# Keys and values of batches 2 to 7: half of each group of eight is added by an accumulating DMA from GpSimd

## The chip, the cores and the metric

The kernel runs on one core of a Trainium2 chip. The core has five engines that work side by side, each through its own instructions in program order: TensorE (PE, matrix products, with PEld for its weight loads), VectorE (DVE), ScalarE (ACT), GpSimd (POOL) and SyncE (SP). Semaphores order them against each other. Data travel between the chip's memory (HBM) and the on-chip SBUF by DMA; TensorE writes its products to PSUM, the second on-chip memory. The metric is the time of one execution in microseconds. Three runs of the kernel before took 1375.69, 1375.94 and 1376.54 us; their median, 1375.94, is the time before.

## What is computed

The reference is an attention whose keys and values are averaged over groups of eight positions, followed by two feed-forward layers. Cut to what matters:

```python
# q, k, v: 8 batches x 8 heads x 576 positions x 64
k_p = k.reshape(B, H, 72, 8, 64).mean(axis=3)
v_p = v.reshape(B, H, 72, 8, 64).mean(axis=3)
scores = q @ k_p.transpose(0, 1, 3, 2) / 8
attn = softmax(scores)                      # with 1e-9 in the denominator
x = (attn @ v_p)                            # as 4608 tokens x 512
h = x @ w_in                                # 512 x 2048
g = maximum(h, 0) + log1p(exp(-abs(h)))
x = g @ w_out                               # 2048 x 512
# second layer: each token goes to one of 8 experts (the largest of its logits)
out[mask] = gate * (maximum(x[mask] @ w1[e], 0) @ w2[e])
```

The sums over eight positions (`k_p`, `v_p`) are the part that the change is about. Each (head, pooled position) has 8 x 64 = 512 numbers that lie in HBM one after the other; the sum over the eight leaves 64.

## The kernel before, in words

The 4608 tokens are cut into nine blocks of 512. For each block, `mm1` multiplies by `w_in` in 16 chunks of 128 columns, `softplus` forms `g` on ScalarE and VectorE, and `mm2` multiplies by `w_out` into four PSUM accumulators. Each float32 product is made of three products of split halves (`three`, lines 656 to 658). The attention of a later batch runs between the chunks of an earlier block: transposes of queries (`Q`, line 321), scores (`S`, line 338, tile `pp`), transposes of the attention weights (`T`, lines 395 and 401, tiles `pm` and `pl`) and the products with the values (`AV`, lines 422 to 425, tile `pv`). In this stage the tiles `pq`, `pp`, `pm`, `pl` and `pv` share two PSUM buffers (tag `a`), so TensorE can begin one only when the one before the last has been read out.

Batches 0 and 1 are prepared in the first block, by a list of steps written out by hand (`ORDER`, line 1182). Batches 2 to 7 are prepared by a planner (`make_plan`), which puts steps into the gaps between the chunks of the blocks 1 to 8. Its steps for a batch are `FK` and `FV` (the loads of keys and values), `PK` (sum the keys over eight and multiply by two masks), `KT` (transpose them), `PV` and `PR` (sum the values) and `BV` (masks and splits of the values).

- A batch's keys are loaded by SyncE in three DMAs: two of 128 x 2 x 512 (`fetch_main`, line 225) and one of 64 x 512 with the rows that don't fit (`fetch_kl`, line 236). Its values take five: two of 128 x 2 x 512 (line 225) and three copies of 32 x 2 x 512 (`fetch_vl`, line 245).
- All go to a pool `stp` of three buffers (tag `st`). A buffer is loaded again only when the sums that read it are done; SyncE waits for that in its queue, and what is behind it in the queue waits too.
- VectorE sums over eight: `pool_sum`, line 186, one instruction for each of the eleven pieces of a batch: four of `ks`, one of `klm`, four of `vs`, two of `vl`. The two pieces of `vl` hold 96 rows, the one of `klm` 64.
- GpSimd multiplies by the masks (line 219, tiles `km`, `vm`, `vlm`), scales the attention weights (line 358, tile `e`), and in block 1 subtracts to split every other chunk of `w_out` (line 638, tile `wo`; VectorE has the rest). VectorE then spreads a part of `e` into `el` (line 369); both are transposed by TensorE.

TensorE and SyncE run in the order in which the program text issues their instructions. VectorE, ScalarE and GpSimd run, from block 1 on, in an order that a scheduler chose when the kernel was built; it is fixed in the program, and on the chip each engine keeps to it.

Of the kernel before, what the change touches and what calls it, by code (L numbers as in the profile page):

```python
# [9 lines left out]
F32 = mybir.dt.float32  # L10
# [3 lines left out]
ALU = mybir.AluOpType  # L14
AX = mybir.AxisListType
# [5 lines left out]
def tile_attention_moe_moe(  # L21
# [13 lines left out]
    nc = tc.nc  # L35
    P = 128
    B, H, S, D = q.shape
    POOL = 8
# [4 lines left out]
    NJ = H // 2  # L43
# [8 lines left out]
    PK = 2 * SP  # L52
# [8 lines left out]
    stp = ctx.enter_context(tc.tile_pool(name="stp", bufs=3))  # L61
# [121 lines left out]


    def pool_sum(dst, src, pin):
        ins = nc.vector.tensor_reduce(dst, src.rearrange("p (e d) -> p d e", e=POOL), AX.X, ALU.add)
        if pin:
            tc.keep_in_program_order(ins)

    def rows(a, b):  # L190
        return a[b].rearrange("h (s e) d -> (h s) (e d)", e=POOL)


    def stage(shape, dtype, early):
        if early:
            return wp.tile(shape, dtype, tag="W", name="st")
        return stp.tile(shape, dtype, tag="st", name="st")
# [10 lines left out]
    def add(dst, src, step):  # L208
        if alt(step):
            tree_sum(dst, src)  # L210
        else:
            pool_sum(dst, src, int(step[1:step.index(".")]) > 1)
# [7 lines left out]

    km_t, st_t, el_t = {}, {}, {}

    def fetch_main(a, b, i, early):
        st = stage([P, 2, POOL * D], F32, early)
        nc.sync.dma_start(st, rows(a, b).rearrange("(j r) c -> r j c", j=NJ)[0:P, 2 * i:2 * i + 2, :])
        return st

    def fetch_k(b, i):
        st_t["k", b, i] = fetch_main(k, b, i, b < 2)

    def fetch_v(b, i):
        st_t["v", b, i] = fetch_main(v, b, i, b < 2)

    def fetch_kl(b):
        st = stp.tile([P, POOL * D], F32, tag="st", name="st")
        nc.sync.dma_start(st[0:64, :], rows(k, b).rearrange("(j r) c -> r j c", j=NJ)[P:PK])
        st_t["kl", b] = st

    def fetch_vl(b):
        st = stp.tile([P, 2, POOL * D], F32, tag="st", name="st")
        src = rows(v, b).rearrange("(j r) c -> r j c", j=NJ)[P:PK]
        for i in range(3):
            nc.sync.dma_start(st[32 * i:32 * (i + 1)], src)
        for g in range(2):
            st_t["vl", b, g] = st[:, g, :]

# [279 lines left out]
    def emit_step(o):  # L528
        if o[0] == "T":
            run(atrans(o[1]))  # L530
        elif o[0] == "Q":
            t = o[1]
            if t + 1 < NTL:
                load_q(t + 1)
            run(qtrans(t))
        elif o[0] == "S":
            run(score(o[1]))
            run(spread(o[1]))
        elif o[0] == "FK":
            for i in range(2):  # L540
                fetch_k(o[1], i)
            fetch_kl(o[1])
        elif o[0] == "FV":
            for i in range(2):
                fetch_v(o[1], i)
            fetch_vl(o[1])
        elif o[0] in ("PK", "KT", "PV", "PR"):
            if o not in preps:
                preps[o] = {"PK": prep_k, "KT": kT, "PV": prep_v, "PR": prep_r}[o[0]](o[1])
            next(preps[o], None)  # L550
        elif o[0] == "AV":
            _, si, j = o
            run(av(si, j))
        elif o[0] == "BV":
            run(build_r(o[1]))
            run(build_v(o[1]))
# [615 lines left out]
    def loads(c, *a):  # L1172
        f = {"k": fetch_k, "l": fetch_kl, "v": fetch_v, "r": fetch_vl, "q": load_q, "i": fetch_in, "o": fetch_out}
        f[c](*a)
# [218 lines left out]
```

## Time and profile before

The profiled execution took 1376.53 us; its span, from the first to the last instruction, is 1374.70 us, so 1.83 us lie outside the span. It is 0.59 us above the median of the three runs.

| engine | busy, us | share of the span | instructions |
|---|---|---|---|
| PE | 1350.0 | 98% | 6998 |
| DVE | 763.5 | 56% | 1608 |
| ACT | 644.5 | 47% | 1287 |
| POOL | 281.4 | 20% | 268 |

The granted clock of TensorE is 0.996 of its full speed over the span. The chain of work that ended last lies on PE for 83% of the span, on DVE for 8%, on DMA for 3%. A busy share is an average over the span: what an engine's work is worth in one stage is seen only in that stage, by who waits for whom there. All 166.94 MB of DMA traffic but 1.22 MB of instruction code go through SyncE's queue; GpSimd issues none of it.

### The profile page before, as it was taken

The numbers are of one execution on the slowest core, as the hardware profiler recorded it, in microseconds if no ns is written. First come the engines' busy times: TensorE is split into PE (matmuls) and PEld (weight loads), VectorE is DVE, ScalarE is ACT, GpSimd is POOL, SyncE is SP. The second block draws the span as 40 slices with busy tenths as digits, with TensorE's granted clock in tenths as the row PEclk, the third lists the DMA queues.
The fourth block names the chain that finished last, engine by engine and source line by source line (L and its number), as shares of the span: only waits on it lengthen the run. The fifth ranks groups of instructions, "written<-read, shape, count | busy, mean of one in ns | idle before, by whom it ended". The sixth has DMA issues, their size and how long they took to land.

```text
span 1374.7 us, 18505 instructions
## 1 busy us (share of the span) xinstructions
PE 1350.0 (98%) x6998; PEld 1118.0 (81%) x6998; DVE 763.5 (56%) x1608; ACT 644.5 (47%) x1287; POOL 281.4 (20%) x268
## 2 busy tenths in 40 slices
PE   8999999999999999999999999999999999999998
PEld 7666678878888878888888888878878898998986
DVE  7997567566465466475564443353664544544432
ACT  5766455554465464564464454455532322222221
POOL 6500112121021020020020010073353022231100
PEclk9999999999999999999999999999999999999999
DMA  9742354353364363453442242563332212222000
GB/s 275 244 125 85 105 172 140 112 195 107 113 203 124 95 195 92 127 181 95 139 153 85 79 152 77 168 210 126 107 124 93 87 37 77 78 93 93 31 31 32
DMA packets 113564, 166.94 MB, mean 121 GB/s; under 512 B 42808, under 2 KB 69432, under 8 KB 113472
## 3 DMA queue, kind: packets, MB, share of 16 engines
q1 hardware_dynamic: 113472, 165.72, 38.2%
q8 instruction: 57, 0.93, 0.3%
q14 instruction: 35, 0.29, 0.1%
HBM read 128.99 MB, written 36.70 MB: 121 GB/s over the span
## 4 chain that ended last, share of the span: by engine, by line
PE 83%; DVE 8%; DMA 3%; POOL 2%; ACT 2%; issue 1%; SPq 1%; POOLq 0%; DVEq 0%; ACTq 0%
PE h L656 8%; PE h L658 8%; PE h L657 8%; PE acc L656 8%; PE acc L658 8%; PE acc L657 8%; PE y L656 5%; PE y L657 5%; PE y L658 5%; PE m L656 4%; PE m L658 4%; PE m L657 4%; PE pp L338 2%; PE acc L710 2%; PE lg L742 1%; DMA wos<-wo 1%
## 5 line engine op out<-in xcount | busy, mean ns | idle before, releaser
L656 PE MATMUL h<-x,wi 128*128 128x512 f32 x576 | 234.9, 408 | 1.2 <-DVE t L689 1.1
L658 PE MATMUL h<-x,wi 128*128 128x512 f32 x576 | 225.7, 392 | 0.0
L657 PE MATMUL h<-x,wi 128*128 128x512 f32 x576 | 225.0, 391 | 0.0
L672 ACT ACTIVATE t<-h 128x512 f32<-128x512 f32 x144 | 86.1, 598 | 229.5 <-PE h L658 222.7
L656 PE MATMUL acc<-g,ring 128*128 128x512 f32 x448 | 177.9, 397 | 0.1
L658 PE MATMUL acc<-g,ring 128*128 128x512 f32 x448 | 174.8, 390 | 0.0
L657 PE MATMUL acc<-g,ring 128*128 128x512 f32 x448 | 174.4, 389 | 0.0
L689 DVE SCALAR_TENSOR_TENSOR t<-h,t 128x512 f32<-128x512 f32 x128 | 87.9, 687 | 147.3 <-ACT t L676 146.1
L656 PEld LDWEIGHTS h<-x,wi 128*128 128x128 f32 x576 | 108.7, 189 | 24.4 <-DVE t L689 1.8
L658 PEld LDWEIGHTS h<-x,wi 128*128 128x128 f32 x576 | 108.4, 188 | 24.2
L657 PEld LDWEIGHTS h<-x,wi 128*128 128x128 f32 x576 | 108.8, 189 | 21.1 <-issue 1.0
L691 ACT CAST g<-t 128x512 fp32r<-128x512 f32 x128 | 79.6, 622 | 86.7 <-DVE t L689 86.6
L693 DVE TENSOR_TENSOR g<-t,g 128x512 fp32r<-128x512 f32 x128 | 92.0, 719 | 50.7 <-ACT g L691 50.6
L656 PE MATMUL y<-w,g 128*128 128x512 f32 x288 | 113.0, 392 | 0.0
L657 PE MATMUL y<-w,g 128*128 128x512 f32 x288 | 112.9, 392 | 0.0
L658 PE MATMUL y<-w,g 128*128 128x512 f32 x288 | 112.9, 392 | 0.0
L658 PEld LDWEIGHTS acc<-g,ring 128*128 128x128 f32 x448 | 84.1, 188 | 18.4
L656 PEld LDWEIGHTS acc<-g,ring 128*128 128x128 f32 x448 | 84.2, 188 | 16.2 <-issue 0.6
L657 PEld LDWEIGHTS acc<-g,ring 128*128 128x128 f32 x448 | 84.2, 188 | 15.8
L358 POOL TENSOR_TENSOR e<-e,sm 128x576 f32<-128x576 f32 x34 | 39.4, 1159 | 270.9 <-DVE sm L355 223.5
L676 ACT ACTIVATE t<-t 128x512 f32<-128x512 f32 x144 | 91.4, 635 | 2.9
L674 ACT ACTIVATE t<-t 128x512 f32<-128x512 f32 x144 | 91.5, 636 | 2.1
(228 smaller groups left out, 2713.9 us busy)
## 6 DMA issues: line engine op xcount, KB each, us to landing
ring<-wos SPq DMA_DIRECT2D x112, 512.0 KB, 3.7
x2s<-x SPq DMA_DIRECT2D x9, 2048.0 KB, 8.3
b<-x2s SPq DMA_DIRECT2D x27, 512.0 KB, 5.2
out_dram<-o SPq DMA_DIRECT2D x36, 256.0 KB, 2.1
st<-in_k_dram SPq DMA_DIRECT2D x16, 512.0 KB, 5.1
q<-in_q_dram SPq DMA_DIRECT2D x32, 256.0 KB, 4.3
st<-in_v_dram SPq DMA_DIRECT2D x16, 512.0 KB, 6.7
st<-in_moe_w_in_dram SPq DMA_DIRECT2D x16, 512.0 KB, 7.0
```

The lines of the kernel that those rows point to most:

```text
L338: nc.tensor.matmul(pp[p0:p0 + n, i, :], qT[:, j, p0:p0 + n], kbd_t[b][:, j, :], start=True, stop=True)
L358: eng.tensor_tensor(e, e, sm1.unsqueeze(2).to_broadcast([P, H, SP]), ALU.mult)
L656: nc.tensor.matmul(ps, ll, rh, start=first, stop=False, skip_group_check=more)
L657: nc.tensor.matmul(ps, lh, rl, start=False, stop=False, skip_group_check=more)
L658: nc.tensor.matmul(ps, lh, rh, start=False, stop=last, skip_group_check=more)
L672: nc.scalar.activation(t, h, AF.Abs)
L674: nc.scalar.activation(t, t, AF.Exp, scale=-1.0)
L676: nc.scalar.activation(t, t, AF.Ln, bias=1.0)
L689: nc.vector.scalar_tensor_tensor(t, h, 0.0, t, ALU.max, ALU.add)
L691: nc.scalar.copy(g[:, 0, :], t)
L693: nc.vector.tensor_tensor(g[:, 1, :], t, f32(g)[:, 0, :], ALU.subtract)
L710: nc.tensor.matmul(accs[blk][d], wof[fc][:, dd], f32(g)[:, 0, :], start=first, stop=(fc == NFC - 1))
```

## The change

For batches 2 to 7 each staging buffer is half as wide. SyncE loads the first four of each eight positions into it (256 numbers for a row). When these have landed, GpSimd issues a second DMA that reads the other four positions from HBM and adds them in SBUF to what lies there (`accum_op=ALU.add`). VectorE sums four values instead of eight. Batches 0 and 1 are loaded and summed as before. The view in `pool_sum` is written by its inner size (`d=D`), so that it takes four or eight.

```diff
     def pool_sum(dst, src, pin):
-        ins = nc.vector.tensor_reduce(dst, src.rearrange("p (e d) -> p d e", e=POOL), AX.X, ALU.add)
+        ins = nc.vector.tensor_reduce(dst, src.rearrange("p (e d) -> p d e", d=D), AX.X, ALU.add)
...
+    HALF = POOL * D // 2
+
+    def added(dst, src):
+        nc.sync.dma_start(dst, src[..., 0:HALF])
+        nc.gpsimd.dma_start(dst, src[..., HALF:], accum_op=ALU.add)
+
     def fetch_main(a, b, i, early):
-        st = stage([P, 2, POOL * D], F32, early)
-        nc.sync.dma_start(st, rows(a, b).rearrange("(j r) c -> r j c", j=NJ)[0:P, 2 * i:2 * i + 2, :])
+        st = stage([P, 2, POOL * D if early else HALF], F32, early)
+        src = rows(a, b).rearrange("(j r) c -> r j c", j=NJ)[0:P, 2 * i:2 * i + 2, :]
+        if early:
+            nc.sync.dma_start(st, src)
+        else:
+            added(st, src)
         return st
...
     def fetch_kl(b):
-        st = stp.tile([P, POOL * D], F32, tag="st", name="st")
-        nc.sync.dma_start(st[0:64, :], rows(k, b).rearrange("(j r) c -> r j c", j=NJ)[P:PK])
+        st = stp.tile([P, POOL * D if b < 2 else HALF], F32, tag="st", name="st")
+        src = rows(k, b).rearrange("(j r) c -> r j c", j=NJ)[P:PK]
+        if b < 2:
+            nc.sync.dma_start(st[0:64, :], src)
+        else:
+            added(st[0:64, :], src)
         st_t["kl", b] = st
...
     def fetch_vl(b):
-        st = stp.tile([P, 2, POOL * D], F32, tag="st", name="st")
+        st = stp.tile([P, 2, POOL * D if b < 2 else HALF], F32, tag="st", name="st")
         src = rows(v, b).rearrange("(j r) c -> r j c", j=NJ)[P:PK]
         for i in range(3):
-            nc.sync.dma_start(st[32 * i:32 * (i + 1)], src)
+            if b < 2:
+                nc.sync.dma_start(st[32 * i:32 * (i + 1)], src)
+            else:
+                added(st[32 * i:32 * (i + 1)], src)
```

A batch then has eight accumulating DMAs on GpSimd, 48 in all. Lines after the change stand 17 higher from line 268 on (358 is 375, 638 is 655, 693 is 710); the new DMAs are lines 226 (SyncE) and 227 (GpSimd). TensorE's and SyncE's instructions keep their order. The scheduler's orders of the other three change at a few places.

The first place is GpSimd's queue where the values of batch 3 are fetched. Before, it holds the masks of the keys, two pieces of `w_out` and one tile of attention weights:

```order
L358 TENSOR_TENSOR e_2105<-e_2105,sm_2118 128x576
L219 TENSOR_SCALAR km_2279<-ks_2210,hm 128x4x64 x2
L638 TENSOR_TENSOR wo_2323<-wof_123,wo_2323 128x512
L358 TENSOR_TENSOR e_2281<-e_2281,sm_2294 128x576
L638 TENSOR_TENSOR wo_2465<-wof_123,wo_2465 128x512
```

Now, in the same place (`e_2105` is `e_2116`, `e_2281` is `e_2292`; numbers behind a name count buffers):

```order
L375 TENSOR_TENSOR e_2116<-e_2116,sm_2129 128x576
L219 TENSOR_SCALAR km_2290<-ks_2221,hm 128x4x64 x2
L227 DMA st<-in_v_dram 128x2x256 x2
L655 TENSOR_TENSOR wo_2334<-wof_123,wo_2334 128x512
L227 DMA st<-in_v_dram 32x2x256 x3
L375 TENSOR_TENSOR e_2292<-e_2292,sm_2305 128x576
L655 TENSOR_TENSOR wo_2481<-wof_123,wo_2481 128x512
```

Two accumulating DMAs now stand ahead of a piece of `w_out`, and three more ahead of the attention weights `e_2292`.

The second place is VectorE's queue where the values of batch 2 are summed, at the end of a token block's routing. Before:

```order
L799 RECIPROCAL gate_all<-n 128x4
L638 TENSOR_TENSOR wo_1957<-wof_122,wo_1957 128x512
L186 TENSOR_REDUCE vs_1821<-st 128x64
L693 TENSOR_TENSOR g<-t,g 128x512
L186 TENSOR_REDUCE vs_1821<-st 128x64
L438 TENSOR_TENSOR x_1905<-pv,x_1905 128x128 x3
```

Now:

```order
L816 RECIPROCAL gate_all<-n 128x4
L710 TENSOR_TENSOR g<-t,g 128x512
L186 TENSOR_REDUCE vs_1829<-st 128x64
L655 TENSOR_TENSOR wo_1965<-wof_122,wo_1965 128x512
L186 TENSOR_REDUCE vs_1829<-st 128x64
L455 TENSOR_TENSOR x_1913<-pv,x_1913 128x128 x3
```

The subtraction that ends `g` has changed places with the piece of `w_out`; the same two sums stand ahead of the read-out of `pv`.

The third place is GpSimd's queue where the keys of batch 4 are fetched. Before:

```order
L219 TENSOR_SCALAR vlm_3140<-vl_2787,lm 96x128 x2
L219 TENSOR_SCALAR vm_3145<-vs_2648,hm 128x4x64 x2
L768 TENSOR_TENSOR n<-lt,half 128x4
L358 TENSOR_TENSOR e_2932<-e_2932,sm_2945 128x576
L358 TENSOR_TENSOR e_3097<-e_3097,sm_3110 128x576
```

Now:

```order
L219 TENSOR_SCALAR vlm_3159<-vl_2803,lm 96x128 x2
L219 TENSOR_SCALAR vm_3164<-vs_2664,hm 128x4x64 x2
L227 DMA st<-in_k_dram 128x2x256 x2
L227 DMA st<-in_k_dram 64x1x256
L785 TENSOR_TENSOR n<-lt,half 128x4
L375 TENSOR_TENSOR e_2951<-e_2951,sm_2964 128x576
L375 TENSOR_TENSOR e_3116<-e_3116,sm_3129 128x576
```

The three accumulating DMAs of the keys stand behind the masks of the values of batch 3, and ahead of a routing step. The batches 5 to 7 look alike.

## Rows read from the trace of the kernel before

**Rows 1.** Busy time by stretch: start and end, length, engines, clock, DMA share, GB/s.

```profile
133.00:725.00 592.00, 587.12 (x2862) 474.94 (x2861) 351.76 (x714) 312.24 (x599) 97.58 (x92) 1.00 0.44 138
```

**Rows 2.** Line 186 alone in that stretch: length, DVE busy and count.

```profile
133.00:725.00 592.00, 69.34 (x66) 1.00 0.44 138
```

**Rows 3.** Groups by line in that stretch, DVE: busy, mean ns, idle before.

```profile
L344 DVE TENSOR_REDUCE mx<-pp 128x4 f32<-128x288 f32 x50 | 22.3, 453 | 21.7 <-PE pp L338 21.4
...
L351 DVE TENSOR_REDUCE sm<-e 128x8 f32<-128x576 f32 x25 | 18.8, 751 | 10.6 <-ACT e L348 10.6
...
L778 DVE TENSOR_REDUCE m<-z 128x4 f32<-128x32 f32 x5 | 0.9, 186 | 0.2
```

**Rows 4.** Timeline of PE, four waits: start, length, instruction, idle before and releaser.

```profile
206.03 0.33 PE L422 MATMUL pv<-aH,VL 128*128 128x128 f32 x1 [1.24 <-DVE x L438]
...
236.07 0.30 PE L395 MATMUL pm<-ident,e 128*128 128x128 f32 x1 [0.33 <-DVE x L438]
...
489.71 0.36 PE L338 MATMUL pp<-kbd,qT 128*128 128x144 f32 x1 [1.53 <-DVE aL L407]
...
703.73 0.36 PE L338 MATMUL pp<-kbd,qT 128*128 128x144 f32 x1 [0.55 <-DVE aL L407]
```

**Rows 5.** Timeline of DVE ahead of the first of these waits.

```profile
202.59 0.68 DVE L638 TENSOR_TENSOR wo<-wof,wo 128x512 fp32r<-128x512 f32 x1
...
205.69 0.48 DVE L438 TENSOR_TENSOR x<-pv,x 128x128 fp32r<-128x128 f32 x2
```

**Rows 6.** Timeline of ACT in the same stretch.

```profile
202.09 0.62 ACT L691 CAST g<-t 128x512 fp32r<-128x512 f32 x1 [0.29 <-DVE t L689]
```

**Rows 7.** Timeline of DVE ahead of the third and fourth wait.

```profile
487.75 1.04 DVE L186 TENSOR_REDUCE vs<-st 128x64 f32<-128x512 f32 x1
...
701.30 1.09 DVE L186 TENSOR_REDUCE vs<-st 128x64 f32<-128x512 f32 x1
```

**Rows 8.** Timeline of SP's queue: the values of batch 3.

```profile
234.02 1.98 SPq L225 DMA_DIRECT2D st<-in_v_dram  x2
239.67 1.95 SPq L245 DMA_DIRECT2D st<-in_v_dram  x3
```

**Rows 9.** Lines 225 and 245: issue in ns, and us to landing (min/median/max).

```profile
L225 SPq DMA_DIRECT2D st<-in_k_dram x16: 378/424/585, 0.7 to 605.3; - x16
...
DMA to landing us min/median/max: 3.5/5.7/10.3
...
DMA to landing us min/median/max: 2.7/6.1/7.2
```

**Rows 10.** Groups by line in the stretch 133 to 725, POOL.

```profile
L768 POOL TENSOR_TENSOR n<-lt,half 128x4 f32<-128x4 f32 x5 | 5.2, 1047 | 57.5 <-DVE lt L765 40.5 <-DVE sm L353 17.0
```

**Rows 11.** Timeline of POOL at the values of batch 3.

```profile
235.76 2.38 POOL L219 TENSOR_SCALAR km<-ks,hm 128x256 f32<-128x256 f32 x2 [6.42 <-DVE ks L186]
240.87 1.30 POOL L638 TENSOR_TENSOR wo<-wof,wo 128x512 fp32r<-128x512 f32 x1 [2.73 <-ACT wo L634]
245.65 1.15 POOL L358 TENSOR_TENSOR e<-e,sm 128x576 f32<-128x576 f32 x1 [3.48 <-ACT qT L324]
```

**Rows 12.** Timeline of DVE behind that.

```profile
246.83 0.42 DVE L369 COPY el<-e 128x96 f32<-128x96 f32 x2
247.67 0.22 DVE L276 COPY kbd<-pk 128x64 f32<-128x64 f32 x1 [0.42 <-PE pk L271]
...
249.02 0.48 DVE L438 TENSOR_TENSOR x<-pv,x 128x128 fp32r<-128x128 f32 x2
```

**Rows 13.** Timeline of PE in the same place.

```profile
244.46 0.48 PE L656 MATMUL acc<-g,wo 128*128 128x512 f32 x1
...
251.31 0.22 PE L422 MATMUL pv<-aH,VL 128*128 128x128 f32 x1
```

**Rows 14.** Timeline of POOL where the keys of batch 4 are fetched.

```profile
297.29 1.83 POOL L219 TENSOR_SCALAR vm<-vs,hm 128x256 f32<-128x256 f32 x2
```

**Rows 15.** Timeline of DVE behind the first sum of those keys.

```profile
307.93 0.69 DVE L689 SCALAR_TENSOR_TENSOR t<-h,t 128x512 f32<-128x512 f32 x1 [3.58 <-ACT t L676]
```

## The prediction

> **What bounds the kernel now.** I read the busy time by stretch first. Batches 2 to 7 are prepared between 133 and 725 us. In these 592.00 us TensorE is busy for 587.12, at a granted clock of 1.00; VectorE for 352, ScalarE for 312, GpSimd for 98, and the DMA engines for a share of 0.44 [rows 1]. So TensorE sets the pace here. Work taken from VectorE gives time back only where TensorE waits for VectorE, and all the idle time that TensorE has in this stretch is 592.00 - 587.12 = 4.88 us. That is the most that the change can win. What it can lose has no such limit: each engine works through its queue in order, so an instruction that waits on GpSimd holds all that is behind it.
>
> Next I looked, on the timeline of TensorE, for the waits behind which sums stand. There are four [rows 4]: 1.24 us at 206 (a `pv` waits until VectorE has read out an earlier one), 0.33 at 236, 1.53 at 490 and 0.55 at 704. Together they are 3.65 of the 4.88. Last I read the queues of SyncE and GpSimd at the fetches.
>
> **What the sums cost, and what half of one costs.** Line 186 runs 66 times in the stretch (eleven for each of six batches) for 69.34 us [rows 2], 1.051 us each for 512 elements. Two other reductions, which read neighbouring elements, take 453 ns for 288 elements and 751 for 576 [rows 3]: (751 - 453) / 288 = 1.035 ns an element, and 155 ns fixed. At that rate 512 elements would take 685 ns. The sums take 366 more. Either each element costs more because the sum steps 64 elements at a time, or each of the 64 results costs 366 / 64 = 5.7 ns. By the first reading half the elements save (1051 - 155) / 2 = 448 ns with the fixed part and 525 without; by the second 256 x 1.035 = 265. The small reduction of line 778 has four results from 32 elements: 155 + 33 = 188 ns without a charge for results, 211 with one. It takes 186 [rows 3]. So I take the first reading, in its middle: 0.49 us saved for each sum, and keep 0.27 as the lower end. On VectorE that is 66 x 0.49 = 32 us, nearly all of it beside a busy TensorE and worth nothing.
>
> [...]
>
> **What of it lies on the path.**
> - At 206: two sums stand between the end of the routing and the read-out that is waited for. Before, the piece of `w_out` began at 202.59 and the read-out at 205.69 [rows 5]. Now `g` comes first; it needs ScalarE's cast, which ends at 202.09 + 0.62 = 202.71 [rows 6], 0.12 later than the 202.59. Gain 2 x 0.49 - 0.12 = 0.86 of the 1.24.
> - At 236: four sums stand ahead, 1.96 us shorter together. The whole 0.33 goes.
> - At 490 and 704: I count only the sum that starts at 487.75 and the one at 701.30 [rows 7], with TensorE's wait right behind them: 0.49 each.
>
> Sum of the gains: 0.86 + 0.33 + 0.49 + 0.49 = 2.17 us.
>
> **What the second DMA costs.** The time from issue to landing of such loads is 5.7 us for line 225 and 6.1 for line 245 at the median [rows 9]. I leave these as they are for the halves of SyncE, though they carry half the bytes. GpSimd's DMA waits for that landing, and GpSimd's queue waits with it. No DMA is issued from GpSimd in this trace, so how long one keeps it busy has to be bounded: from below by SyncE's issue, 0.42 us; from above by GpSimd being held until the data are there, 5.7 us [rows 9]. The nearest row is a small instruction of GpSimd itself, line 768, with 1.05 us [rows 10]. I take 1.05.
>
> Behind most fetches GpSimd's next instruction comes many microseconds later. The tight place is batch 3's values. SyncE issues their first two DMAs in 1.98 us from 234.02 [rows 8], the second at about 236.0 - 0.42 = 235.6; they land at 239.7 and 241.3. GpSimd is free from 235.76 + 2.38 = 238.14 [rows 11]. It issues at 239.7 and at 241.3, and starts the piece of `w_out` at 242.35 in place of 240.87. That ends at 243.65; TensorE needs it at 244.46 [rows 13], so this costs nothing. The other three wait for the sum of the odd keys, which is 0.49 shorter: SyncE issues them from 239.67 - 0.49 = 239.2, 0.65 apart [rows 8], and they land from 245.3 to 246.6. GpSimd issues them until 245.3 + 3 x 1.05 = 248.45, and only then scales the attention weights, which it began at 245.65 before [rows 11]: 2.8 us late. VectorE's queue stops at the spread of these weights (`el`), with the read-out of the `pv` tiles behind it at 249.02. VectorE was idle for 0.42 between the two [rows 12], so the read-out starts at 249.02 + 2.8 - 0.42 = 251.4 and has the first tile done half of 0.48 later, at 251.64. TensorE's next `pv` wants that buffer at 251.31 [rows 13]. It waits 0.33.
>
> **Sum.** On the profiled execution: 1376.53 - 2.17 + 0.33 = 1374.69 us. That execution lies 0.59 above the median of the runs, so the forecast for the median is 1374.1, a gain of 0.13%. A measurement of this kernel can tell about 0.2%, 2.75 us, from no change; the forecast lies within it.
>
> **The rivals.**
> 1. *The issue on GpSimd is dear: slower.* Call it c. By the times above, the weights of batch 3 start 3c after the later of 245.3 (the landing) and 239.7 + 2c + 1.3 (two issues and the piece of `w_out`), and TensorE waits for what that lies beyond 251.31 + 0.42 - 0.24 - 249.02 + 245.65 = 248.12. For c = 2 this is 3.2 us, for 2.4 it is 4.9, for 3 it is 7.9. From 2.4 on the loss eats the gain of 2.17 and 2.75 more. With 3 the time is 1375.94 - 2.17 + 7.9 = 1381.7; at the upper bound of 5.7 the wait is 21.4 and the time 1395.2. For it: a second DMA has to read what lies in SBUF, and nothing in the trace shows how that is set up. Against it: instructions of GpSimd on few elements take about 1 us.
>    [...]
> 2. *The data come late.* Batch 4's keys are summed early. GpSimd's masks end at 297.29 + 1.83 = 299.1 [rows 14], two issues later it is 301.2. The shortened sum, 0.56, must be done before VectorE's instruction at 307.93, ahead of which it was idle for 3.58 [rows 15]; so the data have 6.1 us from the issue. With 5.7 they are in time. With the slowest landing seen, 10.3 [rows 9], that instruction starts 4.2 late. TensorE can run ahead by its second `h` buffer; I take half, 2.1 us, and the same at batch 5: 1374.1 + 4.2 = 1378.3.
> 3. *VectorE's relief reaches further.* All idle time of the stretch goes and GpSimd costs nothing: 1375.94 - 4.88 = 1371.1. For it: shorter queues on VectorE help ScalarE and GpSimd too. Against it: more than one microsecond of that idle time has no sum ahead of it.
> 4. *A sum of four is hardly shorter.* With 0.27 saved the gains are 0.42, 0.33, 0.27 and 0.27, together 1.29, and the time is 1375.94 - 1.29 + 0.33 = 1375.0.
>
> **How the numbers follow.** Forecast 0.45, first rival 0.25, second 0.08, third 0.12, fourth 0.10. Faster by over 0.2%: the third and a small part of the forecast, 0.15. Slower: nearly all of the first and half of the second, 0.27. The rest, 0.58, is no change. The range for 8 in 10 reaches from near the third rival, 1371.5, to the first with c = 3, 1382.0; the dear half of the first rival and a little below the third stay out.
>
> **What would show it.** In the profile after: line 186 at about 0.56 us for the 66 sums (0.79 would be the second reading); the wait at 206 near 0.4, those at 490 and 704 smaller; GpSimd's issues about 1 us apart, and the weights of batch 3 two to three microseconds later against TensorE than before; VectorE's sums never waiting for a DMA but at batch 2's keys. Wrong it is if TensorE's idle time between 133 and 725 grows over 4.88 us: then I look for who waits for GpSimd at line 375 or 655, and read c from the queue of GpSimd.

## The result, and the profile after

The changed kernel takes 1390.73 us (median of four runs, 1388.32 to 1392.67), the kernel before 1376.10 in the runs beside it: a ratio of 1.0103, with a 95% interval of 1.0084 to 1.0122. It is slower by 1%, outside the predicted range. The profiled execution took 1392.49 us, its span is 1390.7, 16.0 more than the span before.

The sums did become shorter. Line 186 in the trace after (engine, operation, count, shortest/median/longest in ns, then the idle time of VectorE ahead of them and what ended it):

```profile
L186 DVE TENSOR_REDUCE ks<-st x27: 591/611/1050, 4.5 to 668.4; 128x64 f32<-128x256 f32 x24, 128x64 f32<-128x512 f32 x3
...
L186 DVE TENSOR_REDUCE vl<-st x13: 605/610/1035, 11.5 to 732.8; 96x64 f32<-96x256 f32 x12, 96x64 f32<-96x512 f32 x1
...
  DMA st<-in_k_dram: 25.1, 6
```

A sum of four takes 0.61 us where one of eight took 1.05 [rows 2]: 0.44 saved. But the sums of keys now wait 25.1 us for their data, where they waited 5.5 before. The busy time of the stretch that [rows 1] shows of before:

```profile
133.00:725.00 592.00, 578.70 (x2798) 468.45 (x2797) 321.59 (x705) 306.58 (x589) 144.16 (x136) 0.99 0.48 133
```

TensorE is idle for 592.00 - 578.70 = 13.30 us where it had 4.88, and its clock is no longer 1.00 throughout. TensorE runs the same instructions in the same order in both kernels, so the start of the same matmul in either trace tells where the time goes:

| matmul | before, us | after is behind by |
|---|---|---|
| `h`, ahead of all fetches | 119.83 | +0.95 |
| after the waits at 206 and 236 | 236.91 | -0.45 |
| `pv`, values of batch 3 | 248.07 | +3.03 |
| 13 matmuls later | 250.63 | +5.32 |
| `h`, keys of batch 4 | 309.94 | +6.98 |
| `pp`, keys of batch 5 | 407.90 | +13.03 |
| 16 matmuls later | 411.27 | +15.83 |
| after the wait at 490 | 489.71 | +15.41 |
| after the wait at 704 | 703.73 | +14.72 |
| end of the span | 1374.7 | +16.0 |

The gains stand where the prediction put them: 1.40 at 206 and 236, 0.42 at 490, 0.69 at 704. Three places lose: 3.48 and then 2.30 at the values of batch 3, 1.65 at the keys of batch 4, 6.05 and then 2.80 at those of batch 5. The 0.95 us ahead of the fetches and the 1.3 between 704 and the end say nothing on the change: in the kernels below, whose work there is nearly the same, these two figures run from -1.9 to +2.4 and from -0.5 to +1.3.

What makes the data late stands in GpSimd's queue. Line 227 holds the accumulating DMAs (the first rows: count, ns as above; then GpSimd's idle time ahead of them, and what ended it; last, from issue to landing):

```profile
L227 POOL DMA_DIRECT2D st<-in_v_dram x30: 1193/1344/1943, 178.6 to 687.2; - x30
L227 POOL DMA_DIRECT2D st<-in_k_dram x18: 837/1253/1422, 138.3 to 633.1; - x18
...
  issue: 47.7, 11
...
DMA to landing us min/median/max: 3.2/5.5/7.1
```

One issue takes 1.25 to 1.34 us at the median, near the 1.05 that was assumed. The news is the line "issue": GpSimd stood still for 47.7 us in eleven times with nothing named to wait for. The one ahead of the very first DMA at 138 us (2.99 us) is no news: SyncE's load of that data was issued at 134.68 and landed 2.86 later, and in the kernel below where GpSimd issues no DMA but adds in SBUF, 2.99 us stand ahead of its first addition as well. The other ten, 3.65 to 5.38 us each, stand ahead of the second large DMA of a fetch, and none ahead of a third. Each of them ends 0.32 to 0.34 us after the first DMA of the fetch has landed: at the keys of batch 5 that one was issued at 406.60 and landed at 411.54, and the second was issued at 411.86. One more, 3.24 us ahead of 214.23, is put down to VectorE's `sm`, but ends 0.32 behind the landing too. At the values of batch 3 (GpSimd's timeline: start, length, instruction, idle before):

```profile
238.89 1.26 POOL L227 DMA_DIRECT2D st<-in_v_dram  x1 [1.38 <-DMA st<-in_v_dram]
244.26 1.19 POOL L227 DMA_DIRECT2D st<-in_v_dram  x1 [4.12 <-issue]
245.00 1.78 POOL L655 TENSOR_TENSOR wo<-wof,wo 128x512 fp32r<-128x512 f32 x1
246.24 3.05 POOL L227 DMA_DIRECT2D st<-in_v_dram  x3
247.94 2.52 POOL L375 TENSOR_TENSOR e<-e,sm 128x576 f32<-128x576 f32 x1
```

The weights `e` started at 245.65 before [rows 11]; now they end at 250.46. VectorE's `el` waits 2.90 for them. Behind `el` in VectorE's queue stands the copy of `pk` to `kbd`, and `pk` is one more of the tiles that share the two PSUM buffers of tag `a`. For the buffer that this copy frees TensorE stands still for 3.38; the read-out of `pv` at 252.16 comes later still. VectorE, then TensorE:

```profile
250.50 0.41 DVE L386 COPY el<-e 128x96 f32<-128x96 f32 x2 [2.90 <-POOL e L375]
250.83 0.21 DVE L293 COPY kbd<-pk 128x64 f32<-128x64 f32 x1
...
252.16 0.68 DVE L455 TENSOR_TENSOR x<-pv,x 128x128 fp32r<-128x128 f32 x2
```

```profile
251.10 0.48 PE L439 MATMUL pv<-aH,VL 128*128 128x128 f32 x1 [3.38 <-DVE kbd L293]
...
252.54 0.63 PE L674 MATMUL h<-x,wi 128*128 128x512 f32 x1
252.97 0.63 PE L675 MATMUL h<-x,wi 128*128 128x512 f32 x1
...
256.36 0.40 PE L674 MATMUL h<-x,wi 128*128 128x512 f32 x1
256.59 0.39 PE L675 MATMUL h<-x,wi 128*128 128x512 f32 x1
```

Behind the wait the matmuls start 0.43 us apart until 256, and 0.23 apart from then on. The granted clock (third figure from the end of a row) was half of full there, and again in and behind the wait at 415; at 427 it is full again:

```profile
253.00:254.00 1.00, 1.00 (x4) 0.81 (x3) 0.00 (x0) 0.00 (x0) 0.00 (x0) 0.50 0.91 365
...
418.00:419.00 1.00, 0.00 (x0) 0.00 (x0) 0.57 (x1) 0.00 (x0) 0.00 (x0) 0.50 0.08 11
424.00:425.00 1.00, 1.00 (x3) 0.76 (x3) 0.93 (x3) 0.00 (x0) 0.00 (x0) 0.50 0.00 0
427.00:428.00 1.00, 1.00 (x5) 0.81 (x5) 0.00 (x0) 0.67 (x2) 0.00 (x0) 1.00 0.00 0
```

The clock fell within an idle time of 3.4 us (0.75 in the microsecond from 249, 0.50 from 250 on) and of 6.3 us (0.87 in that from 416, 0.50 from 417 on), and rose while matmuls ran (0.84 in that from 256, 1.00 from 427 on). This is the 2.30 and the 2.80 of the table. At the keys of batch 5 the chain can be read across four engines:

```profile
406.60 1.27 POOL L227 DMA_DIRECT2D st<-in_k_dram  x1 [3.91 <-DMA st<-in_k_dram]
411.86 2.10 POOL L227 DMA_DIRECT2D st<-in_k_dram  x2 [3.99 <-issue]
```

```profile
418.43 0.60 DVE L186 TENSOR_REDUCE ks<-st 128x64 f32<-128x256 f32 x1 [9.25 <-DMA st<-in_k_dram]
419.06 0.69 DVE L706 SCALAR_TENSOR_TENSOR t<-h,t 128x512 f32<-128x512 f32 x1
```

```profile
419.79 0.62 ACT L708 CAST g<-t 128x512 fp32r<-128x512 f32 x1 [8.67 <-DVE t L706]
420.31 0.57 ACT L773 COPY l<-lg 32x512 f32<-32x512 f32 x1
```

```profile
420.93 1.32 PE L355 MATMUL pp<-kbd,qT 128*128 128x144 f32 x4 [6.26 <-ACT l L773]
```

The profile names ScalarE's `l` as what TensorE waited for. It is only the last link: `l` stood behind `g`, that behind VectorE's `t`, that behind a sum of keys, and this waited 9.25 us for a DMA that GpSimd had issued after a pause.

### The profile page after: what moved, and what is told of

Its sections match the earlier page's. It is cut to its first block, busy times and chain, and to the rows that moved or that the text cites. A ratio compares the mean times of both kernels' runs of the same rounds, so it can differ in the third digit from the quotient of the medians.

```text
span 1390.7 us, 18644 instructions
## 1 busy us (share of the span) xinstructions
PE 1356.2 (98%) x6998; PEld 1122.9 (81%) x6998; DVE 737.3 (53%) x1608; ACT 644.2 (46%) x1287; POOL 331.2 (24%) x316
## 3 DMA queue, kind: packets, MB, share of 16 engines
q0 software_dynamic: 8448, 7.87, 3.9%
## 4 chain that ended last, share of the span: by engine, by line
PE 79%; DVE 7%; DMA 6%; POOL 2%; issue 2%; ACT 2%; SPq 1%; POOLq 0%; DVEq 0%; ACTq 0%
PE h L673 8%; PE h L675 8%; PE h L674 8%; PE acc L673 7%; PE acc L675 7%; PE acc L674 7%; PE y L673 5%; PE y L674 5%; PE y L675 5%; PE m L673 4%; PE m L675 4%; PE m L674 4%; PE acc L727 2%; PE pp L355 2%; DMA st<-in_k_dram 2%
## 5 line engine op out<-in xcount | busy, mean ns | idle before, releaser
L673 PEld LDWEIGHTS h<-x,wi 128*128 128x128 f32 x576 | 110.0, 191 | 24.9 <-DVE t L706 1.9
L675 PEld LDWEIGHTS h<-x,wi 128*128 128x128 f32 x576 | 109.7, 190 | 24.6
L674 PEld LDWEIGHTS h<-x,wi 128*128 128x128 f32 x576 | 110.1, 191 | 21.5 <-issue 1.0
```

Of the source, the lines that this page charges most:

```text
L673: nc.tensor.matmul(ps, ll, rh, start=first, stop=False, skip_group_check=more)
L674: nc.tensor.matmul(ps, lh, rl, start=False, stop=False, skip_group_check=more)
L675: nc.tensor.matmul(ps, lh, rh, start=False, stop=last, skip_group_check=more)
```

## The experiments

The theories. A: the pause is missing room. This program sets aside 1024 bytes per partition of SBUF for GpSimd's DMAs (`dynamic_dma_scratch_size`), and the second large accumulating DMA finds no room until the first has drained. What lies in that room no trace shows. That the pauses end 0.32 to 0.34 us after the first DMA has landed fits A, and B as well. B: two accumulations are kept from overlapping, whatever the room. C: every issue is dear by itself, the first rival of the prediction.

**More room, everything else alike.** The order of all engines is that of the changed kernel.

```diff
-    nc = _bacc.Bacc(..., dynamic_dma_scratch_size=1024)
+    nc = _bacc.Bacc(..., dynamic_dma_scratch_size=1536)
-        vl = kp.tile([96, 2, D], F32, tag="vl", name=f"vl{b}")
+        vl = kp.tile([96, 2, D], F32, tag="ks", name=f"vl{b}")
```

> The changed kernel with one and a half times the memory for GpSimd's DMA descriptors (1536 bytes per partition instead of 1024; the order of every engine is unchanged; the vl tile shares a buffer with ks to make room). In the changed kernel GpSimd sits idle for 47.7 us in 11 times, 3.0 to 5.4 us each, with nothing shown to wait for, always ahead of the second accumulating DMA of a fetch and never ahead of the third. Theory A (no room for the second DMA's descriptors until the first has drained): the 47.7 us fall under 5, the sums of the odd keys and values get their data about 4 us earlier, TensorE's waits at 248 (3.4 us) and 310 go and the one at 408 (6.3) falls to 2 to 3; time 1378 to 1383. Theory B (two accumulating DMAs are kept from overlapping, whatever the room): the pauses stay at 3 to 5.4 us, time 1390 to 1393. Theory C (the first rival of the prediction, every issue is dear on GpSimd by itself): the pauses stay, 1390 to 1393.

Measured: 1377.51 us, ratio to before 0.9998 (0.9988 to 1.0009). GpSimd's idle time ahead of line 227 that the page puts down to "issue" (2.96 of it ahead of the very first DMA), and the values of batch 3:

```profile
  issue: 3.3, 2
```

```profile
239.65 2.48 POOL L227 DMA_DIRECT2D st<-in_v_dram  x2 [1.39 <-DMA st<-in_v_dram]
241.41 2.03 POOL L655 TENSOR_TENSOR wo<-wof,wo 128x512 fp32r<-128x512 f32 x1
243.30 0.94 POOL L227 DMA_DIRECT2D st<-in_v_dram  x1
245.22 1.66 POOL L227 DMA_DIRECT2D st<-in_v_dram  x2 [0.98 <-DMA st<-in_v_dram]
247.00 1.15 POOL L375 TENSOR_TENSOR e<-e,sm 128x576 f32<-128x576 f32 x1
```

The two DMAs now follow each other at once, and the 14 us are gone. Of the waits 0.86 us is left at 408. A holds, B and C fall: the same 48 accumulating DMAs, now of 1.56 us at the median, don't pause. They aren't free: from 120 to 704 TensorE gains 2.14 us on the kernel before, against 3.54 with no second DMA (below). The time came out a little below what A gave (1378 to 1383).

**Plain copies.** `accum_op=ALU.add` is left out; the sums then lack half of their values.

> The changed kernel with GpSimd's DMAs as plain copies that don't add (the second half replaces the first, so the sums lack the first four positions of each eight; the order of work is the same). [...] Theory A (room for descriptors): two plain copies fit, the pause ahead of the second goes, the time is 1378 to 1383 as with more room. Theory B (accumulations don't overlap): the pause goes as well, and the landing may be shorter than the 5.5 us of the changed kernel. Theory C (each issue is dear on GpSimd): the pause stays at 3 to 5 us and the time at 1388 to 1393.

Measured: 1372.63 us, ratio 0.9970 (0.9961 to 0.9979). The pauses are gone but for 0.19 to 0.35 us in five places. An issue takes 0.55 to 0.73 us at the median and lands after 4.0. The row of GpSimd's queue in either page (packets, MB, share of the DMA engines), first the changed kernel, then this one:

```profile
q0 software_dynamic: 8448, 7.87, 3.9%
```

```profile
q0 software_dynamic: 2688, 7.87, 1.8%
```

Adding made 8448 packets of 7.87 MB here, the plain copies 2688 of the same bytes. The forecast of the time was too high: it took over the loss from late data that is left with accumulating DMAs and more room. There VectorE's sums of keys wait 14.4 us, here 8.9.

**The relief alone.** GpSimd's DMA is taken out; four of each eight positions are left out of the sums.

> The changed kernel without GpSimd's DMAs: SyncE loads the first four of each eight positions and VectorE sums these (the other four are left out of the sums of batches 2 to 7). This is the relief of VectorE and half the traffic, without the cost of the second DMA. The prediction's sum gives a gain of 2.17 us over the kernel before, so 1373.8; its third rival, that all idle time of TensorE from 133 to 725 goes, gives 1371. If VectorE's relief is worth nothing on the path: 1375.5 to 1376.5.

Measured: 1372.68 us, ratio 0.9977 (0.9967 to 0.9987), so 3.2 us faster, with 1.8 to 4.5 in the interval. In the trace TensorE gains 3.54 us from 120 to 704, where the prediction had 2.17, and is idle for 1.99:

```profile
133.00:725.00 592.00, 590.01 (x2879) 477.98 (x2878) 324.64 (x714) 313.66 (x601) 96.76 (x92) 1.00 0.41 125
```

**The values alone.** Keys are loaded whole.

```diff
-        st_t["k", b, i] = fetch_main(k, b, i, b < 2)
+        st_t["k", b, i] = fetch_main(k, b, i, b < 2, True)   # True: all eight positions by SyncE
```

> The change for the values alone; the keys of batches 2 to 7 are loaded whole by SyncE and summed over eight as in the kernel before. Against the kernel before, TensorE in the changed kernel falls behind by 5.8 us at the values of batch 3 (3.5 us of waiting and 2.3 behind it with matmuls at half pace), by 1.7 at the keys of batch 4 and by 8.8 at the keys of batch 5. If these are separate mechanisms, the two at the keys (10.5 us) go and the one at the values stays: 1380 to 1382. If the loss at the keys is only moved to other places, it stays at 1388 or more.

Measured: 1377.66 us, ratio 1.0009 (0.9999 to 1.0019). The losses at the keys are gone, so they are not merely moved. At the values of batch 3 it lost 1.72 us, not the 5.8 expected, and again for the copy to `kbd`:

```profile
PE pv L436 <- DVE kbd L290: 1.6, 1, 1.6
```

The pause is still there (3.55 us), but the first DMA went out at 237.76, 1.13 earlier than in the changed kernel, and the wait of 1.6 was not followed by matmuls at half pace.

**How much room.** The only edit is 1088 bytes for 1024.

> The changed kernel with 1088 bytes per partition for the descriptors in place of 1024, and nothing else. More room took the pause away in the run before this one; the question is how much is short. [...]

Measured: 1374.85 us, ratio 0.9983 (0.9972 to 0.9993). The keys of batch 5:

```profile
398.80 2.52 POOL L227 DMA_DIRECT2D st<-in_k_dram  x2 [3.91 <-DMA st<-in_k_dram]
404.01 0.83 POOL L227 DMA_DIRECT2D st<-in_k_dram  x1 [2.69 <-issue]
```

With 64 bytes more the second large DMA follows at once, and the pause stands ahead of the third. By A, 1024 bytes are then short of two by 64 or less; what one DMA takes of the room no run shows. With 1536 bytes none of the five DMAs of the values paused for "issue". The third DMA carries the small rest, which is summed last; there the pause hurts little: TensorE falls behind by 0.92 at the keys of batch 5, where it was 6.05.

**The small one in the middle**, at the old 1024 bytes: the lines `fetch_k(b, 1)` and `fetch_kl(b)` change places.

> The changed kernel at the old 1024 bytes, with the keys' small DMA (64x256) issued between the two large ones. [...] If the engine has to pause after every first DMA, whatever its size: the pause stays ahead of the second. The values are as in the changed kernel. Time 1386 to 1393 either way.

Measured: 1387.18 us in both of two runs, ratio 1.0074 (1.0053 to 1.0095). The same place:

```profile
401.60 2.16 POOL L227 DMA_DIRECT2D st<-in_k_dram  x2 [3.33 <-DMA st<-in_k_dram]
407.53 1.24 POOL L227 DMA_DIRECT2D st<-in_k_dram  x1 [3.76 <-issue]
```

The small DMA followed the first at once, and the pause has moved to the third, now the second large one. It is not tied to the second place in the queue, which fits A.

**Sums further behind their loads**: 1536 bytes and `LEAD = 9`.

> More room (1536 bytes) and the sums of batches 3 to 7 two gaps later behind their loads (LEAD 9 in place of 7). With more room alone VectorE still waited 14.4 us, 5.0 at the longest, in 4 sums of keys for their data, and TensorE 0.9 at 408. If the data's being late is what is left, these waits go and the time is 1375 to 1376.5, a little under the kernel before. If they cost nothing, or the later sums collide with something else: 1377 to 1380.

Measured: 1376.67 us, ratio 0.9997 (0.9988 to 1.0007). The wait at 408 is gone, VectorE's wait for keys is down to 7.7 us in two sums, and TensorE got one of 1.0 us elsewhere. No difference from the run with room alone can be told.

**GpSimd adds in SBUF, no second DMA.**

```diff
+    def folded(x):
+        nc.gpsimd.tensor_tensor(x[..., 0:HALF], x[..., 0:HALF], x[..., HALF:], ALU.add)
+        return x[..., 0:HALF]
```

> Another way to the same relief: SyncE loads all eight positions as in the kernel before, GpSimd adds the second half to the first in SBUF by one addition for each load (128x2x256, 64x256, 96x2x256), VectorE sums four. No DMA from GpSimd. An addition of 512 elements on GpSimd took 1.3 to 1.5 us (the piece of w_out), so the data are ready 1.5 us after the load lands, not 1.3 + 5.5. If the gain of summing four holds (1372.7 without any second DMA, a ratio of 0.9977) and GpSimd's additions hide: 1372 to 1374. If GpSimd's queue holds the attention weights up at batch 3, or its additions slow VectorE beside them: 1375 to 1379.

Measured: 1373.65 us, ratio 0.9978 (0.9968 to 0.9987): faster than the kernel before. The additions, and the stretch of [rows 1]:

```profile
L229 POOL TENSOR_TENSOR st<-st x36: 718/1294/1785, 139.2 to 666.1; 128x512 f32<-128x512 f32 x24, 64x256 f32<-64x256 f32 x6, 96x512 f32<-96x512 f32 x6
```

```profile
133.00:725.00 592.00, 589.89 (x2876) 477.57 (x2876) 334.76 (x718) 314.32 (x602) 143.93 (x128) 1.00 0.45 138
```

TensorE's idle time, 2.11 us, is nearly that of the relief alone. GpSimd had the time, and its addition (1.29 at the median) costs it no more than the issue of an accumulating DMA, without the 5.5 us to the landing.

**Room from elsewhere.** With 1536 bytes the first run had a ratio of 0.9998, with 1088 it was 0.9983, though their intervals overlap. In the first `vl` and `ks` shared a buffer, and at 15 us, in the first block, GpSimd stood still ahead of a `ks`:

```profile
16.81 0.32 POOL L202 TENSOR_TENSOR ks<-st 128x64 f32<-128x64 f32 x1 [1.76 <-issue]
```

```diff
-        vl = kp.tile([96, 2, D], F32, tag="ks", name=f"vl{b}")
+        vl = (sm if b < 2 else kp).tile([96, 2, D], F32, tag="lt" if b < 2 else "ks", name=f"vl{b}")
```

> More room for the descriptors (1536 bytes) as in the run without pauses, but the vl tile of batches 0 and 1 lies in a buffer of the routing that is idle then, and only that of batches 2 to 7 shares one with ks. In the earlier run with 1536 bytes GpSimd stood still for 1.76 us at 15 to 17 us, ahead of a ks of batch 1 whose buffer vl of batch 0 still held, and TensorE waited for GpSimd's weights at 20 us. If this sharing is why 1536 bytes (ratio 0.9998) did less than 1088 (0.9983), the stop at 15 us goes and the time is 1374.5 to 1376 (ratio 0.998 to 0.999). If the difference lay in the later stages or in nothing but scatter: a ratio of 0.9995 to 1.0005.

Measured: 1374.68 us, ratio 0.9987 (0.9979 to 0.9996). The stop at 15 us is gone and the ratio is the one expected. That the stop made the difference is not shown. The intervals of the two runs overlap; and from 20 to 55 us TensorE falls behind by 1.82 in the first run and not at all in this one, but by 1.80 and 2.40 in the changed kernel and the one with GpSimd's additions, where the two tiles share no buffer. Single traces also differ from each other in the first 55 us, where TensorE waits 3.1 us for loads of `q` in the kernel before, by up to 2.5 us to either side; such a difference says nothing on the edit.

## Why the prediction was wrong

- *TensorE sets the pace; at most 4.88 us to win.* Right. The relief alone left 1.99 of them.
- *A sum of four saves 0.49, 0.448 at the low end of the first reading.* 0.44 was measured, just under that end. The first reading was right in kind: 256 elements took 0.61 us, where the second reading gave 0.79.
- *Gains of 2.17.* In the changed kernel's trace 1.40 + 0.42 + 0.69 = 2.51, at the four places named. Without GpSimd's DMAs 3.54.
- *c = 1.05.* 1.19 to 1.42 for a DMA of 128x2x256; 0.85 for 64x256 where it is issued alone. Nothing between 0.42 and 5.7 as a price for each DMA describes what happened, though. **This is the step that failed**: "from above by GpSimd being held until the data are there" was taken as a bound on one number c, applied to every issue alike, and the middle was filled from a row of a small arithmetic instruction. The runs show two things in its place: a small price for each issue, and a pause of 3.65 to 5.38 us ahead of the second large one, which ended 0.32 to 0.34 us after the first had landed. With 64 bytes more room it moved from the second DMA to the third, and the time fell to 0.9983 of that of the kernel before.
- *Batch 3's values: `e` at 248.45, TensorE waits 0.33.* This step failed too. In the changed kernel `e` starts at 247.94, which is 248.45 by the clock of the trace before (TensorE is 0.51 ahead there), just as forecast; yet TensorE lost 3.48. The prediction took the read-out of `pv` for what TensorE waits for, and its next use at 251.31 [rows 13]. The copy of `pk` to `kbd` at 247.67 [rows 12] stands closer behind `el`, and TensorE wanted that buffer 3.24 us earlier:

```profile
248.07 0.27 PE L422 MATMUL pv<-aH,VL 128*128 128x128 f32 x1
```

In the trace after, that matmul starts 0.60 us after `el` begins. With `e` until 248.45 + 1.15 = 249.60 this gives 250.2, an estimate: 2.1 us of waiting and not 0.33. The first rival's 248.12 lies too late by the difference, 1.8. The rest of the 3.48 is `e` itself, which took 2.52 in place of 1.15 while DMAs were issued. That `e` started when it was forecast is luck: the three small loads of SyncE landed after 2.7 to 4.3 us, not 6.1, and the pause made up for it. With room, `e` started at 247.00 and TensorE fell behind by 0.42, near the 0.33 by the same two errors against each other.
- *The forecast of 1374.1, a ratio of 0.9987.* With room it is about met: 0.9983 with 1088 bytes, 0.9987 with 1536 and room from elsewhere, but 0.9998 with 1536 in the first of the experiments. In part this is luck: the relief was worth more than 2.17 (3.54), and the accumulating DMAs cost more than 0.33 (1.4 to 1.9 of the 3.54).
- *First rival.* Its sign was right, and its place was one of three; its mechanism was not: with 1.56 us an issue and no pause the loss was small. An issue of 3 us, with which its loss and the upper end of the range were reckoned, no run shows; the longest took 2.36.
- *Second rival, chance 0.08.* Late data at the keys bore most of the loss: 6.05 and the 2.80 behind it at batch 5 and 1.65 at batch 4, out of 16.3. The pause came on top of the two issues that it counted. It asked only whether one landing could be slow, and not when GpSimd would get to issue.
- *The clock.* The prediction took every wait at its own length. Waits of 3.4 and 6.3 us brought another 2.30 and 2.80 behind them. A wait of 1.6, with the values alone, brought none.
- *What would show it.* "Wrong it is if TensorE's idle time between 133 and 725 grows over 4.88" pointed at the right engine. Of the two lines named with it, 375 was the one at batch 3; the larger loss, at the keys, came by the sums of line 186 that waited for the data of line 227.

## What to carry to other kernels

Before several DMAs are put on GpSimd, ask whether the first will have landed when the next is to start, and try them with more room: here GpSimd stood still for 3.65 to 5.38 us between two large adding ones at 1024 bytes and not at 1088, while at 1024 behind a first plain one the other four went out with "issue" pauses of 0.35 us at most. The sign of it was a pause named "issue" ahead of the second, which ended 0.32 to 0.34 us after the first had landed. A wait in a queue that carries other engines' work is priced by what stands behind it in the queue, and it can cost again by the clock: here a granted 0.50 behind idle times of TensorE of 3.4 and 6.3 us, for another 2.30 and 2.80. When the time behind a wait is priced, follow every tile that shares the buffers, not only the one in view. Where an engine with idle time could do the same addition in SBUF, as GpSimd here, it had the data sooner than a second transfer: 1.29 us at the median, against 1.25 to 1.34 for the issue and 5.5 from issue to landing.

## What was not expected of the hardware

- 64 bytes of room moved the pause. With 1024 bytes per partition an adding DMA of 64x256 followed one of 128x2x256 at once, while GpSimd paused ahead of a second one of 128x2x256, in the changed kernel for 3.65 to 5.38 us; with 1088 the second followed at once, and GpSimd paused ahead of the small one, for 2.69 at the keys of batch 5.
- A DMA that adds moved 7.87 MB in 8448 packets, a plain one in 2688; its issue took 1.25 to 1.34 us at the median against 0.55 to 0.73, its landing 5.5 against 4.0.
- Two operations beside GpSimd's issues grew long: at 244.40 VectorE's scaling of `sm` (0.17 us at the median) took 2.41, and `e`, 1.15 us otherwise, took 2.52 while three DMAs were issued. What held them was not tried.

```profile
244.40 2.41 DVE L370 TENSOR_SCALAR sm<-sm 128x8 f32<-128x8 f32 x1
```
